# Moving set 2's background windows and lengthening the pause after a set's first pair rows

## The chip, the cores and the metric

One Trainium2 chip, one of its cores. The metric is the device time of one execution in microseconds (us), lower is better. The core has a matrix engine (PE), a vector engine (DVE), a scalar engine (ACT), a general engine (POOL) and a DMA-issuing queue (SP, "SPq" in the trace); each works its instructions off in program order and waits where an operand is not ready. ACT and POOL can start transfers too; here POOL starts those of the weights and of the `arena` stores.

## The reference

Four batches of eight heads (32 head streams), 768 tokens, head width 40. For each head a 40x40 state is carried along the tokens, and its readings are the tokens' rows of a two-layer feed-forward block:

```python
for t in range(S):
    y[:, :, t] = einsum('bhd,bhde->bhe', r_t, state)
    Sa = einsum('bhde,bhe->bhd', state, a_t)
    state = state * w_t - einsum('bhd,bhe->bhde', Sa, b_t) + einsum('bhd,bhe->bhde', v_t, k_t)
x = y as (tokens, 320)
h = x @ w_in                      # 3072 x 2048
g = h if h >= 1; 0 if h <= -1; else (h + 1)**2 / 4
out = g @ w_out                   # 3072 x 320
```

## The kernel before, in words

The tokens go in 24 **chunks** of 32 steps, each in two halves of 16 heads, so that one chunk's recurrence becomes a handful of small matrix products (lines 482 to 584: `p`, `cg`, `ss`, `x`, `pr`), with one inverse of a 32x32 unit triangular matrix per head and chunk (`tinv`). Four chunks are a **set**, numbered 0 to 5. What does not depend on the state is done a set ahead, in the background, in three jobs per set:

- **rows** (`prelude`, lines 249 to 301, four parts): loads of w, a, k, b (`ld_w`, `ld_a`, `ld_k`, `ld_b`, L261, SP), a copy to `wz` on ACT (L269), two scans and two small operations on DVE (L245, L277, L278), a copy into `arena` on ACT (L279), three products into `arena` on POOL (L280, L289, L296), and one transfer of `arena` to the DRAM buffer `scr` of that set (L297, POOL). `arena` and `wz` exist once, so part p+1's L279 waits until part p's `arena` has left, and part p+1's L269 until part p's L296 has read `wz`.
- **ab** (`ab_set`, lines 315 to 345): per chunk one load of the pair rows from `scr` into `tiab` (four transfers, L313, SP), then per half two transposes `ea` on DVE (L326), 32 small matmuls on PE (L335), and their copy to `pairs` on ACT (L341). `tiab` exists once: the next chunk's load waits for the last transposes of the chunk before. For set 2 two pads of `tiab` on ACT (L120) come ahead.
- **inv** (`invert`, L347): one transpose of `pairs` on DVE (L351), then 31 pairs of operations on POOL (L362, L368). At the set's first chunk `adopt` (L372) takes the result.

The feed-forward block runs beside it, from the readings of earlier chunks: groups of 64 tokens, each in eight steps of 16 matmuls on PE (L628), the gate on ACT and DVE (L636, L637, L639), a split of `gt` into `gh` (ACT, L645) and `gl` (POOL, L646), and 12 matmuls on PE (L658, eight from `gh`, four from `gl`). A group's readings are relaid by SP into `X0` or `X1` (`X<-Y`, L602, L608, L611), its result is stored by SP (L663). Until about 221 us `X1` also serves as scratch for turning the weights into their high and low parts (ACT L720, L724, L740; DVE L728; POOL L741).

What sets the order is a generator scheme. Each job is a generator whose `yield`s name costs, and `background(n)` steps, at point n (ten units to a chunk), whichever job is most behind its share of its window:

```python
due.append((key, s, at, size[key] * (gone(n) - gone(a)) / (gone(b) - gone(a))))
...
key, _, at, _ = max(due, key=lambda x: x[3] - x[2][0])
at[0] += next(back[key])
```

`WINDOWS` gives a and b per job and set (first entry is set 1), so entry 2 belongs to set 2. A larger cost at a `yield` makes the job count as further on, hence leaves it alone for longer; the size of a job is the sum of its costs. In `ab_set` the pause between the first load of a set and its first transposes is one such cost:

```python
load_rows(tiab, 4 * s, O_A, 80)
yield AB_W[5]
...
if c < 4 * s + 3:
    load_rows(tiab, c + 1, O_A, 80)
    yield AB_W[4]
```

A window only moves the *program order* on each engine; how long anything takes is the chip's.

Of the kernel before, what the change touches and what calls it, by code (L numbers as in the profile page):

```python
# [25 lines left out]


WINDOWS = dict(
    rows=[(0, 0), (24, 43), (46, 64), (70, 90), (106, 130)],
    ab=[(0, 0), (46, 55), (68, 84), (95, 119), (135, 159)],  # L30
    inv=[(5, 36), (55.5, 79), (85, 118), (121, 158), (161, 198)],
)

AHEAD = 5
# [3 lines left out]
SLOTS = len(SHARE)  # L38

ROWS_W = (2, 2, 4, 2, 6, 6, 8)  # L40
AB_W = (1, 16, 1, 4, 46, 40)
INV_W = 12

TRAIL = 2.5
# [10 lines left out]
def rwkv_moe_kernel(ctx: ExitStack, tc: tile.TileContext, r, k, v, w, a, b, w_in, w_out, ident_d, mask_d, out):  # L55
# [247 lines left out]
    def load_rows(dst, c, off, n, h0=0, nh=NH):  # L303

        sc = scr[c // 4]
        for f in range(2):
            for q in range(2):
                row = (h0 + f) * 128 + 32 * (c % 4)
                m = n - 32 * q
                src = bass.AP(  # L310
                    sc.tensor, sc.offset + row * RW + off + 32 * q, [[RW, 32], [256 * RW, nh // 2], [1, m]]
                )
                nc.sync.dma_start(dst[64 * f + 32 * q : 64 * f + 32 * q + 32, :, 0:m], src)  # L313

    def ab_set(s):
# [3 lines left out]
        load_rows(tiab, 4 * s, O_A, 80)  # L319
        yield AB_W[5]  # L320
        for c in range(4 * s, 4 * s + 4):
            tv = tiab.rearrange("p h (j x) -> p h j x", x=40)[:, :, :, 0:32]
            for half in range(2):
                ea = work.tile([128, 8, 2, 32], F32, tag="ea", name="ea")
                for i in range(2):
                    nc.vector.transpose(ea[:, 4 * i : 4 * i + 4], tv[:, 8 * half + 4 * i : 8 * half + 4 * i + 4])  # L326
                    yield AB_W[0]
                yield AB_W[1]
                ps = psum()[:, 0:128]
# [11 lines left out]
                nc.scalar.copy(pairs_f[:, at : at + 128], ps)  # L341
                yield AB_W[2] + AB_W[3]
# [4 lines that stand above are left out]
# [32 lines left out]
    def staged(key, needs, work_of):  # L379
        for s in range(2 if key != "inv" else 0, NS):  # L380
            if needs:
                drain(needs, s)
            total = 0
            for d in work_of(s):
                total += d
                yield d
            if s:
                size[key] = total
            done[key] = s
            yield 0  # L390

    turned_in, turned_out = set(), set()
    done, size, spent = dict(rows=1, ab=1), dict(rows=10 + 4 * (1 + sum(ROWS_W)), ab=AB_W[5] + 3 * AB_W[4] + 8 * (2 * AB_W[0] + sum(AB_W[1:4])), inv=INV_W + 67), {}
    back = {k: staged(*a) for k, a in dict(
# [570 lines left out]
```

## Time and profile before

| | |
|---|---|
| time, median of 3 runs | 860.29 us (860.02 to 860.31) |
| the profiled execution: its own time | 861.24 us |
| its span, first to last instruction | 859.4 us |
| mean granted PE clock | 0.883 of full |
| busy share PE / DVE / ACT / POOL | 80% / 69% / 49% / 51% |

The sum in the prediction is made in the profiled execution's time, which lies 0.95 us above the median of the timed runs; 1.84 us of it are around the span. A busy share is an average: PE is nearly always busy in the last third and has its holes before.

### The profile page before, as it was taken

The numbers are of one execution on the slowest core, as the hardware profiler recorded it, in microseconds if no ns is written. First come the engines' busy times: TensorE is split into PE (matmuls) and PEld (weight loads), VectorE is DVE, ScalarE is ACT, GpSimd is POOL, SyncE is SP. The second block draws the span as 40 slices with busy tenths as digits, with TensorE's granted clock in tenths as the row PEclk, the third lists the DMA queues.
The fourth block names the chain that finished last, engine by engine and source line by source line (L and its number), as shares of the span: only waits on it lengthen the run. The fifth ranks groups of instructions, "written<-read, shape, count | busy, mean of one in ns | idle before, by whom it ended". The sixth has DMA issues, their size and how long they took to land.

```text
span 859.4 us, 35431 instructions
## 1 busy us (share of the span) xinstructions
PE 690.8 (80%) x15360; PEld 633.3 (74%) x15360; DVE 594.3 (69%) x1338; ACT 417.5 (49%) x888; POOL 441.8 (51%) x621
## 2 busy tenths in 40 slices
PE   4225656687567877878998889999999999999994
PEld 4224545576456866768887789898898999999994
DVE  6895689888556845787677797677876778676210
ACT  6306455557433533445545455455455555555552
POOL 0300279986232677845678548674267742222331
PEclk9665656788786989879999799999999999999998
DMA  8999599987598666986858976667354456350100
GB/s 291 188 198 233 95 194 206 217 196 184 130 172 149 152 156 112 181 189 150 165 127 165 190 179 154 131 130 134 85 111 89 98 106 131 84 119 23 36 16 16
DMA packets 221459, 122.01 MB, mean 142 GB/s; under 512 B 142144, under 2 KB 214016, under 8 KB 221304
## 3 DMA queue, kind: packets, MB, share of 16 engines
q1 hardware_dynamic: 215032, 98.12, 56.6%
q0 software_dynamic: 6272, 21.63, 9.4%
q8 instruction: 121, 1.98, 1.1%
q14 instruction: 34, 0.28, 0.1%
HBM read 90.54 MB, written 27.53 MB: 137 GB/s over the span
## 4 chain that ended last, share of the span: by engine, by line
PE 42%; DMA 10%; DVE 6%; POOL 5%; ACT 3%; SPq 3%; issue 2%; ACTq 0%; DVEq 0%; POOLq 0%
PE ph L628 14%; PE po L658 13%; PE p L553 4%; DMA ti<-scr 3%; PE p L542 3%; SPq L313 3%; DMA tiab<-scr 2%; PE p L516 2%; PE p L582 2%; PE p L482 2%; PE p L526 2%; DMA ld_b<-in_b_dram 2%; DMA scr<-arena 2%; POOL gl L646 1%; POOL lw L368 1%
## 5 line engine op out<-in xcount | busy, mean ns | idle before, releaser
L646 POOL TENSOR_TENSOR gl<-gt,gh 128x512 fp32r<-128x512 f32 x96 | 123.8, 1290 | 204.5 <-ACT gh L645 204.5
L628 PE MATMUL ph<-X,w 120*128 120x256 f32 x1536 | 219.1, 296 | 1.2 <-issue 1.2
L628 PEld LDWEIGHTS ph<-X,w 120*128 120x128 f32 x1536 | 198.7, 198 | 8.3 <-issue 1.7
L658 PE MATMUL po<-w,gh 128*128 128x320 f32 x768 | 135.9, 320 | 19.8 <-ACT gh L645 19.8
L658 PEld LDWEIGHTS po<-w,gh 128*128 128x128 f32 x768 | 117.4, 193 | 23.8 <-ACT gh L645 23.1
L639 DVE SCALAR_TENSOR_TENSOR gt<-gt,ph 128x512 f32<-128x512 f32 x96 | 65.7, 684 | 96.2 <-ACT gt L637 87.2
L537 ACT ACTIVATE cg<-p 32x160 f32<-32x160 f32 x192 | 56.5, 295 | 92.5 <-PE p L526 58.8
L658 PE MATMUL po<-w,gl 128*128 128x320 f32 x384 | 79.7, 332 | 20.7 <-POOL gl L646 20.7
L560 DVE SCALAR_TENSOR_TENSOR cg<-p,pr 40x160 f32<-40x160 f32 x184 | 59.1, 321 | 50.8 <-PE p L553 48.7
L636 ACT ACTIVATE gt<-ph,half_c 128x512 f32<-128x512 f32 x96 | 66.0, 688 | 58.0 <-PE ph L628 58.0
L368 POOL TENSOR_TENSOR lw<-lw 128x31 f32<-128x31 f32 (+15 forms) x155 | 86.6, 559 | 9.4
L362 POOL TENSOR_TENSOR lw<-lw 128x31 f32<-128x31 f32 (+15 forms) x155 | 84.0, 542 | 8.9
L494 DVE TENSOR_TENSOR cg<-p,mask 32x256 f32<-32x256 f32 x192 | 80.6, 420 | 3.5
L658 PEld LDWEIGHTS po<-w,gl 128*128 128x128 f32 x384 | 63.7, 201 | 25.3 <-POOL gl L646 24.9
L553 PE MATMUL p<-cg 128*64 128x72 f32 (+1 forms) x1536 | 66.0, 245 | 0.0
L645 ACT CAST gh<-gt 128x512 fp32r<-128x512 f32 x96 | 59.6, 621 | 10.5 <-DVE gt L639 9.5
L547 ACT COPY ss<-p 40x320 f32<-40x320 f32 x92 | 38.6, 419 | 48.7 <-PE p L542 47.2
L637 ACT ACTIVATE gt<-gt 128x512 f32<-128x512 f32 x96 | 60.7, 632 | 3.1
L553 PEld LDWEIGHTS p<-cg 128*64 128x64 f32 x1536 | 60.4, 154 | 0.4 <-issue 0.4
L533 DVE SCALAR_TENSOR_TENSOR cg<-p,mask 32x128 f32<-32x128 f32 x192 | 55.3, 288 | 6.3 <-PE p L526 1.1
L582 PEld LDWEIGHTS p<-pr,ss 40*40 40x40 f32 x1472 | 35.9, 129 | 30.1 <-issue 23.1
L582 PE MATMUL p<-pr,ss 40*40 40x32 f32 x1472 | 40.9, 210 | 21.1 <-DVE pr L466 16.3
(94 smaller groups left out, 1058.9 us busy)
## 6 DMA issues: line engine op xcount, KB each, us to landing
ti<-scr SPq DMA_DIRECT2D x96, 200.0 KB
ti<-scr SPq DMA_DIRECT2D x96, 168.0 KB
scr<-arena POOLq DMA_DIRECT2D x16, 640.0 KB, 6.4
cg<-scr SPq DMA_DIRECT2D x96, 80.0 KB
X<-Y SPq DMA_DIRECT2D x36, 160.0 KB
scr<-wide SPq DMA_DIRECT2D x8, 640.0 KB
w<-in_moe_w_out_dram POOLq DMA_DIRECT2D x16, 320.0 KB, 5.2
tiab<-scr SPq DMA_DIRECT2D x32, 160.0 KB
```

What stands on the lines that cost most here:

```text
L362: eng.tensor_mul(t3, W3[:, 0:n, j : j + 1].broadcast_to([128, n, m]), L3[:, j + 1 :, j].unsqueeze(1).broadcast_to([128, n, m]),)
L368: eng.tensor_sub(W3[:, 0:n, j + 1 :], W3[:, 0:n, j + 1 :], t3)
L494: nc.vector.tensor_tensor(out=cg[q, f::2, C_X : C_X + 64][:, 4 * i : 4 * i + 4].rearrange("p h (j x) -> p h j x", x=32), in0=ps[quarter(f, ...
L553: nc.tensor.matmul(psv[h // 8][64 * f : 64 * f + 64, h // 2 % 4, 0:n3], lhsT=cgw[:, h * CW + C_G : h * CW + C_G + 64], rhs=cg[:, h, C_R : ...
L582: nc.tensor.matmul(psv[er[f], p, :], lhsT=ss[er[f], p, :], rhs=pn[er[f], p, 0, 8:40], start=True, stop=True)
L628: nc.tensor.matmul(phs[k % 2][:, n * j : n * j + n], lhsT=wt[0, f // 4, wi // 2][:, wi % 2, fs], rhs=Xs[g][:, xi, :], start=i == 0, stop=i ...
L636: nc.scalar.activation(gt, ph, AF.Relu, bias=half_c, scale=0.5)
L637: nc.scalar.activation(gt, gt, AF.Square)
L639: nc.vector.scalar_tensor_tensor(out=gt, in0=gt, scalar=1.0, in1=ph, op0=ALU.min, op1=ALU.max)
L645: nc.scalar.copy(gh, gt)
L646: nc.gpsimd.tensor_sub(gl, gt, gh.bitcast(F32))
L658: nc.tensor.matmul(pos[i], lhsT=x[:, ts_], rhs=w, start=q == 0 and k == 0, stop=end)
```

## The change

Only the table is edited. Set 2's rows go from 24–43 to 23–41 units (start a tenth of a chunk sooner, end a fifth sooner), its pair rows from 46–55 to 44–57, its inverse from 55.5–79 to 57.5–79; set 3's pair rows start one unit sooner. The cost after the first `tiab` load goes from 40 to 100, in every set from 2 on, so the ab job's size goes from 362 to 422.

```diff
 WINDOWS = dict(
-    rows=[(0, 0), (24, 43), (46, 64), (70, 90), (106, 130)],
-    ab=[(0, 0), (46, 55), (68, 84), (95, 119), (135, 159)],
-    inv=[(5, 36), (55.5, 79), (85, 118), (121, 158), (161, 198)],
+    rows=[(0, 0), (23, 41), (46, 64), (70, 90), (106, 130)],
+    ab=[(0, 0), (44, 57), (67, 84), (95, 119), (135, 159)],
+    inv=[(5, 36), (57.5, 79), (85, 118), (121, 158), (161, 198)],
...
-AB_W = (1, 16, 1, 4, 46, 40)
+AB_W = (1, 16, 1, 4, 46, 100)
```

No instruction is added or removed; they stand in another order. Three places, on two engines, follow (`scr2` is the buffer of set 2, `scr3` of set 3).

SP, where set 2's first pair rows (chunk 8) are loaded. Before:

```order
L602 DMA X1_2929<-Y_618 40x1024 x3
L608 DMA X1_2929<-Y_618 40x2x256 x2
L611 DMA X1_2929<-Y_618 40x2x256
L313 DMA tiab_81<-scr2_107 32x16x80
L313 DMA tiab_81<-scr2_107 32x16x48
L313 DMA tiab_81<-scr2_107 32x16x80
L313 DMA tiab_81<-scr2_107 32x16x48
L261 DMA ld_w_3029<-in_w_dram 128x1x320
```

And after the change:

```order
L313 DMA tiab_81<-scr2_107 32x16x80
L313 DMA tiab_81<-scr2_107 32x16x48
L313 DMA tiab_81<-scr2_107 32x16x80
L313 DMA tiab_81<-scr2_107 32x16x48
L602 DMA X1_2935<-Y_618 40x1024 x3
L608 DMA X1_2935<-Y_618 40x2x256 x2
L611 DMA X1_2935<-Y_618 40x2x256
L261 DMA ld_w_3029<-in_w_dram 128x1x320
```

The load has moved ahead of the relayout of `X1`; set 3's `ld_w` stands behind both, as before.

DVE, around the transposes of set 2's second and third loads (`ea<-tiab`; chunks 9 and 10). Before:

```order
L466 STREAM_TRANSPOSE pr2_90<-ti1_83 128x16x32
L326 STREAM_TRANSPOSE ea_3346<-tiab_81 128x256 x2
L326 STREAM_TRANSPOSE ea_3386<-tiab_81 128x256 x2
L326 STREAM_TRANSPOSE ea_3414<-tiab_81 128x256 x2
L245 SCALAR_TENSOR_TENSOR ld_w_3224<-wz_79,dz_80 128x400
L277 COPY dz_80<-ld_w_3224 128x40
L278 RECIPROCAL dz_80<-ld_w_3224 128x40
L245 SCALAR_TENSOR_TENSOR wz_79<-wz_79,dz_80 128x400
L639 SCALAR_TENSOR_TENSOR gt_3418<-gt_3418,ph1_64 128x512
L584 SCALAR_TENSOR_TENSOR cg2_87<-p2_3463,pr0_88 40x8x32 x2
```

And after the change:

```order
L466 STREAM_TRANSPOSE pr2_90<-ti1_83 128x16x32
L326 STREAM_TRANSPOSE ea_3327<-tiab_81 128x256 x2
L326 STREAM_TRANSPOSE ea_3361<-tiab_81 128x256 x2
L245 SCALAR_TENSOR_TENSOR ld_w_3224<-wz_79,dz_80 128x400
L277 COPY dz_80<-ld_w_3224 128x40
L278 RECIPROCAL dz_80<-ld_w_3224 128x40
L245 SCALAR_TENSOR_TENSOR wz_79<-wz_79,dz_80 128x400
L639 SCALAR_TENSOR_TENSOR gt_3394<-gt_3394,ph1_64 128x512
L326 STREAM_TRANSPOSE ea_3414<-tiab_81 128x256 x2
L584 SCALAR_TENSOR_TENSOR cg2_87<-p2_3420,pr0_88 40x8x32 x2
```

Before, the first row of `ea` behind L466 is chunk 9's second half and the next two are chunk 10's; after, both rows behind L466 are chunk 9's, and chunk 10's first half comes behind the scans and the gate operation L639. Its second half is now behind `cg<-ti` L461, five operations on.

SP, around set 2's fourth load (chunk 11). Before:

```order
L261 DMA ld_k_3411<-in_k_dram 128x1x320
L313 DMA tiab_81<-scr2_107 32x16x80
L313 DMA tiab_81<-scr2_107 32x16x48
L313 DMA tiab_81<-scr2_107 32x16x80
L313 DMA tiab_81<-scr2_107 32x16x48
L142 DMA scr3_108<-in_v_dram 4096x1x40
L261 DMA ld_b_3458<-in_b_dram 128x1x320
L261 DMA ld_w_3461<-in_w_dram 128x1x320
```

And after the change (the copy L142, `ld_b`, `ld_w`, four `ti1` loads and four `cg0` loads now precede these rows):

```order
L445 DMA cg0_85<-scr1_106 32x8x40
L261 DMA ld_a_3555<-in_a_dram 128x1x320
L313 DMA tiab_81<-scr2_107 32x16x80
L313 DMA tiab_81<-scr2_107 32x16x48
L313 DMA tiab_81<-scr2_107 32x16x80
L313 DMA tiab_81<-scr2_107 32x16x48
L261 DMA ld_k_3680<-in_k_dram 128x1x320
```

The fourth load has moved back past eleven transfers, to behind `ld_a`.

On ACT the rows job of set 2 moves too: L269 and L279 of its parts 1 to 3, which stood behind L645 (`gh<-gt`) or close to it, stand a feed-forward step sooner; and the two pads L120 go from behind the L645 at 221.54 us to ahead of the L636 at 218.77 us. In sets 4 and 5 the first transposes of `tiab` on DVE stand one chunk half later behind their load, and the third and fourth loads of `tiab` stand later on SP; in set 4 the fourth goes from ahead of the `ti` and `cg` loads to behind the following `ld_k`, in set 5 from ahead of the `ti` and `cg` loads to behind them.

## Rows read from the trace of the kernel before

**Rows 1.** Busy time by stretch of the span: from and to, length, busy time of PE, its weight loads, DVE, ACT, POOL (instructions), granted PE clock, DMA share, GB/s.

```profile
140.00:225.00 85.00, 61.59 (x1200) 55.08 (x1200) 71.12 (x138) 51.21 (x116) 68.24 (x90) 0.83 0.86 193
225.00:300.00 75.00, 51.64 (x1156) 46.91 (x1160) 46.14 (x99) 26.92 (x60) 27.37 (x33) 0.77 0.76 156
...
620.00:859.00 239.00, 225.61 (x4398) 212.42 (x4392) 137.10 (x328) 123.21 (x255) 97.56 (x120) 0.99 0.35 76
```

**Rows 2.** Waits over the whole span: engine, what waited, for what: us in total, times, longest us.

```profile
DVE ea L326 <- DMA tiab<-scr: 31.3, 6, 13.6
PE p L335 <- DVE ea L326: 29.2, 8, 11.7
ACT arena L279 <- DMA scr<-arena: 14.6, 5, 4.9
```

**Rows 3.** Timeline of PE: start us, us, engine, line and operation, in brackets the idle time before it and what ended it.

```profile
232.43 0.68 PE L335 MATMUL p<-ea 40*32 40x32 f32 x32 [8.25 <-DVE ea L326]
238.31 3.46 PE L628 MATMUL ph<-X,w 120*128 120x256 f32 x16
248.74 0.56 PE L335 MATMUL p<-ea 40*32 40x32 f32 x32 [1.51 <-DVE ea L326]
262.99 0.76 PE L335 MATMUL p<-ea 40*32 40x32 f32 x32 [11.70 <-DVE ea L326]
278.64 2.18 PE L628 MATMUL ph<-X,w 120*128 120x256 f32 x16
310.80 1.43 PE L658 MATMUL po<-w,gl 128*128 128x320 f32 x4 [5.38 <-POOL gl L646]
```

**Rows 4.** Timeline of SP's queue, 221 to 270 us: start us, us to issue, line, transfer, how many.

```profile
221.44 2.46 SPq L602 DMA_DIRECT2D X<-Y  x3
...
225.65 0.77 SPq L611 DMA_DIRECT2D X<-Y  x1
226.59 1.95 SPq L313 DMA_DIRECT2D tiab<-scr  x4
228.58 0.61 SPq L261 DMA_DIRECT2D ld_w<-in_w_dram  x1
...
250.74 6.46 SPq L313 DMA_DIRECT2D tiab<-scr  x4
...
264.62 1.94 SPq L313 DMA_DIRECT2D tiab<-scr  x4
...
277.70 0.54 SPq L261 DMA_DIRECT2D ld_a<-in_a_dram  x1
```

**Rows 5.** Timeline of DVE, same columns as rows 3.

```profile
231.84 0.77 DVE L326 STREAM_TRANSPOSE ea<-tiab 128x256 f32<-128x256 f32 x2 [7.99 <-DMA tiab<-scr]
...
234.72 0.99 DVE L245 TENSOR_TENSOR_SCAN ld_w<-wz,dz 128x400 f32<-128x400 f32 x1
...
262.49 0.77 DVE L326 STREAM_TRANSPOSE ea<-tiab 128x256 f32<-128x256 f32 x2 [13.57 <-DMA tiab<-scr]
...
268.34 0.85 DVE L584 SCALAR_TENSOR_TENSOR cg<-p,pr 40x256 f32<-40x256 f32 x2
...
279.99 0.67 DVE L466 STREAM_TRANSPOSE pr<-ti 128x512 f32<-128x512 f32 x1
```

**Rows 6.** The chain that ended last, 255 to 425 us: start us, us, what.

```profile
255.97 6.39 DMA tiab<-scr
...
421.37 3.95 DMA tiab<-scr
```

**Rows 7.** Timeline of ACT, 156 to 225 us.

```profile
164.30 0.76 ACT L269 COPY wz<-ld_w 128x320 f32<-128x320 f32 x1 [2.12 <-POOL arena L296]
...
170.61 0.78 ACT L279 COPY arena<-ld_w 128x320 f32<-128x320 f32 x1 [4.90 <-DMA scr<-arena]
...
205.08 0.80 ACT L279 COPY arena<-ld_w 128x320 f32<-128x320 f32 x1 [1.29 <-DMA scr<-arena]
...
218.77 0.68 ACT L636 ACTIVATE gt<-ph,half_c 128x512 f32<-128x512 f32 x1
```

**Rows 8.** Transfers of the tile `arena` to DRAM: us from issue to landing; and the page's row of them with the size of one.

```profile
DMA to landing us min/median/max: 4.2/6.4/9.4
scr<-arena POOLq DMA_DIRECT2D x16, 640.0 KB, 6.4
```

**Rows 9.** The page's groups of the inverse's two operations: busy us, mean ns of one, idle before.

```profile
L368 POOL TENSOR_TENSOR lw<-lw 128x31 f32<-128x31 f32 (+15 forms) x155 | 86.6, 559 | 9.4
L362 POOL TENSOR_TENSOR lw<-lw 128x31 f32<-128x31 f32 (+15 forms) x155 | 84.0, 542 | 8.9
```

**Rows 10.** Timeline of DVE in sets 4 and 5, same columns as rows 3.

```profile
425.51 0.77 DVE L326 STREAM_TRANSPOSE ea<-tiab 128x256 f32<-128x256 f32 x2 [3.47 <-DMA tiab<-scr]
...
484.42 0.73 DVE L326 STREAM_TRANSPOSE ea<-tiab 128x256 f32<-128x256 f32 x2
...
544.22 0.77 DVE L326 STREAM_TRANSPOSE ea<-tiab 128x256 f32<-128x256 f32 x2 [3.78 <-DMA tiab<-scr]
```

**Rows 11.** Timeline of PE, behind the first of the waits in rows 10.

```profile
427.77 0.46 PE L335 MATMUL p<-ea 40*32 40x32 f32 x32 [0.24 <-DVE cg L584]
```

**Rows 12.** Timeline of SP's queue around set 4's fourth load.

```profile
467.35 5.38 SPq L313 DMA_DIRECT2D tiab<-scr  x4
...
480.27 0.55 SPq L261 DMA_DIRECT2D ld_k<-in_k_dram  x1
```

## The prediction

> **What bounds the kernel now.** I read the busy time by stretch first. From 620 us on PE is busy for 225.61 of 239 us at a granted clock of 0.99 [rows 1]: no hole to speak of, so whatever comes earlier or later before that point passes one for one to the end. In the stretch 225 to 300 us it is busy for only 51.64 of 75 us, at 0.77 [rows 1]. The change reorders work in and around it. Next the list of waits: DVE waits 31.3 us in six places for the pair rows of `tiab`, and PE 29.2 us in eight places for the transposes made of them [rows 2]. The timeline of PE shows where: 8.25 us before 232.43, 1.51 before 248.74, 11.70 before 262.99, together 21.46 us, all in set 2 [rows 3]. DVE's own waits behind the first and the last of these are 7.99 and 13.57 us, and both end with a landing of `tiab<-scr` [rows 5]. So the hole is two late loads, passed DVE to PE. While it lasts the clock falls to 1.2 GHz: the 16 matmuls at 238.31 take 3.46 us, those at 278.64 take 2.18 [rows 3].
>
> A second wait matters, since the change touches it: ACT waits 14.6 us in five places for `arena` to have left [rows 2].
>
> **First load of set 2 (chunk 8).** Now SP relays `X1` from 221.44 to 226.42, then issues the load at 226.59, and DVE goes on at 231.84 [rows 4, 5], 5.25 us after the first issue. DVE had come to the wait at 231.84 − 7.99 = 223.85. After the change the load stands ahead of the relayout. It then waits for the two pads, which ACT makes just before the L636 at 218.77 [rows 7]; with their 1.2 us and the rows job shifted I put the issue at 220.0 to 222.0, landing 5.25 behind the first issue, at 225.3: a wait of 1.4 us instead of 7.99. That would be 6.6 us, but DVE does not keep it. Behind the transposes comes the scan of set 3's first part, at 234.72, 2.88 us behind 231.84 [rows 5]; it would come to 228.2. Its `ld_w` is issued behind load and relayout in both orders: 228.58 now [rows 4], 227.0 then (222.0 plus the relayout's 4.98). The fastest landing of a comparable transfer is 3.95 us [rows 6], and now at most 234.72 − 228.58 = 6.14 with ACT's copy in it. With 3.95 and a copy of 0.76 [rows 7] the scan starts at 231.7: **−3.0 us**, between −1.6 (6.14) and −6.6 (it has long landed). What stands behind the scan on DVE (L584, then the masks, which PE and ACT wait for) moves with it. So `ld_w` is what is late next.
>
> **Third load (chunk 10).** It keeps its place behind the stores of `ob`; its four issues take 6.46 us from 250.74 because the queue is full [rows 4], and the last lands 6.39 us after 255.97 [rows 6]. It lands about as late as now, less what the stretch before gained. But what stands behind the wait changes: now DVE makes both halves' transposes, two scans, their small operations and a gate operation before it reaches L584 at 268.34, 5.85 us after the wait ended at 262.49 [rows 5]. After the change scans and gate stand ahead of the wait and are made inside it; between the wait and L584 is one pair of transposes, 0.77. So L584, and with it the recurrence, gains 5.08: **−5.0 us**. The bounds: nothing, if the scan's `ld_w` or ACT's copy of it is late too (the second load now stands ahead of that `ld_w` on SP); 11.7, if the wait goes whole. I take the value the DVE rows give, since the load's place on SP is the same. With the stalls shorter by 8 us of some 21, one group of 16 matmuls goes at 2.4 GHz: 3.46 − 2.18, **−1.3 us** (0 to −2.6).
>
> **Fourth load (chunk 11).** Now issued at 264.62, it is never waited for. Afterwards it stands behind the copy of v, four `ti1` and four `cg0` loads and `ld_a`, which goes out at 277.70 today [rows 4], about 9 us sooner by then: issue 269 to 271, landing 5.25 to 8.3 us behind the first issue (1.94 + 6.39 with the third load's landing), at 274.3 to 277.3. Its transposes stand behind the L466 at 279.99 [rows 5], then at 271.4 (279.99 + 0.67 − 9.3). DVE waits 3 to 6 us, and L351, the next scan and the gate with it: **+3.5 us**, between 0 (`ti` and `cg` need less time when the queue is less full) and 6. This is a wait that the change makes.
>
> **The rows job sooner, 150 to 215 us.** ACT makes L269 and L279 of parts 1 to 3 one step ahead. L269 waits for POOL's L296 (2.12 us before 164.30) and L279 for `arena` to leave (4.90 before 170.61, 1.29 before 205.08) [rows 7]. These waits stood behind the L645 of their step; now the L645, the L547 and the weights stand behind them. A transfer of `arena` lands 4.2 to 9.4 us after its issue, 6.4 in the middle [rows 8]. PE is busy for 61.59 of 85 us there [rows 1], so part of it is cover. If each of the three waits for `arena` is one middle landing less what ACT does meanwhile (some 3 us), and half lies in PE's holes, that is 3 × 3.4 / 2 = 5; less what is already paid for two of the parts (4.90 and 1.29, half) 3.1, so 2; with three waits of 2.12 for L296, of which one is paid, another 1: **+3.0 us**, from 0 to 12.7 (three times 2.12 + 4.90, 21.06, less the 8.31 paid today, all of it on PE's path). By the Trainium skill ("DMA: Bandwidth & Descriptors", section "Anatomy of one DMA — SWDGE (gpsimd) path") a transfer that POOL starts takes about 2.0 us and its bytes over 436 GB/s: an estimate of 3.5 us for 655,360 bytes. The trace disagrees: its fastest is 4.2 and its middle 6.4 [rows 8]. By the Trainium skill the waits for `arena` would nearly vanish and the total be some 3 us less; I keep the rows.
>
> **POOL behind set 2's inverse.** At 310.80 PE has waited 5.38 us for `gl` [rows 3], which stood behind operations of the inverse. The inverse starts later, so three of its pairs fewer stand ahead, 3 × (0.559 + 0.542) [rows 9]: **−3.3 us** (0 to −5.4). The same pairs come later in a window of 21.5 units instead of 23.5, up to 340 us, where PE waits for `gl` again: **+1.0 us** (0 to 3.3).
>
> **Sets 3 to 5.** DVE's waits of 3.47 and 3.78 us at the first loads [rows 10] go, as the transposes stand half a chunk later. PE hardly had them: 0.24 us before the products at 427.77 [rows 11]. Against that set 4's fourth load goes from 467.35 to behind `ld_k` at 480.27 [rows 12], and its transposes are due at 484.42 [rows 10]: landing 5.25 us after an issue at 480.8 gives 486.1, a new wait of 1.6 us; set 5 has the like, with more room. **+1.0 us** (−1.5 to +4).
>
> **Sum.** −3.0 − 5.0 − 1.3 + 3.5 + 3.0 − 3.3 + 1.0 + 1.0 = **−4.1 us**: gains of 12.6, losses of 8.5. The profiled execution's 861.24 becomes 857.1, and the timed median, 860.29, becomes **856.2**.
>
> **Rivals.** *The waits go whole.* If the loads land in time everywhere and none is late in their place, PE gets back 21.46 and the clock's 1.3 and POOL's 3.3, less 5.0 of losses without the fourth load's: −21.1, 839.2. For it speaks that the first load has three times its cover; against it that third and fourth load go no sooner on SP. *A new wait takes the place of the old.* `ld_w` of set 3 is as late as `tiab` was (−3.0 becomes 0) and the fourth load costs 6: gains 9.6, losses 11.0, 861.7, within what a measurement can tell from no change. For it speaks that it is the same queue and the same bytes; in that case the change does not do what moving the first load says. *The rows job's ring decides, slower.* With the waits of L269 and L279 all on the path, 12.7 instead of 3.0: 12.6 − 18.2 = −5.6 the wrong way, 865.9. It decides from the point where they cost more than 3.0 + 4.1 + 1.7 = 8.8. For it speaks that each L645 feeds PE directly and ACT is strictly in order; against it that PE had 23 us of holes there anyway. *The stores of `arena` land before ACT asks for them*: the 3.0 of the ring is nothing, 853.2; the fastest landing, 4.2 us [rows 8], is longer than the some 3 us of ACT's work between, so I give it little. (It is what the Trainium skill's figure above would make of it.)
>
> **How the numbers follow.** Two runs of this kernel can be told apart from about 0.2%, 1.7 us. The sum's case has 0.45 (its own range 850 to 858.5), the early landing 0.03, the waits gone whole 0.10; no measurable change 0.18; the ring (or late loads of sets 4 and 5 with it) 0.24. Faster is 0.58, same 0.18, slower 0.24. The range of 847 to 866 leaves out the waits gone nearly whole and the worst of the ring.
>
> **What would show it.** In the trace after: DVE's wait at the first load of set 2 falls below 3 us, and the scan behind it waits for `ld_w`; at the third load DVE still waits for `tiab`, with scan and gate ahead of it; a new wait of 3 to 6 us for `tiab` at the fourth load; ACT's waits at L279 between 155 and 200 us grow and stand ahead of L645; PE's wait before 310 for `gl` shrinks to about 2; around 484 us DVE waits for `tiab`. The prediction is wrong if the third load lands 5 us sooner or later than now apart from the shift, or if the stretch to 225 us ends over 6 us later.

## The result, and the profile after

| | before | after |
|---|---|---|
| median of 13 runs each | 860.31 us (856.06 to 863.92) | 867.03 us (861.53 to 871.52) |
| ratio, 95% interval | | 1.0078 (1.0049 to 1.0107) |
| the profiled execution, its span | 861.24, 859.4 us | 869.86, 868.0 us |

The change makes the kernel 0.8% slower; 856.2 was forecast, with 866 as the upper end. The first three runs of before lay within 0.3 us of each other, thirteen spread over 8: one profiled execution is good to some us, so a reading below counts only where its step is larger than that or is seen in several kernels. The two profiled executions compared here differ by 8.6 us, the medians by 6.7. The ratios of this document leave out two runs that lie over 1.5% above the fastest of their kernel (one of the pause alone, one of the earlier `ld_w` in the changed kernel), so they are not always the quotients of the medians.

Busy time by stretch of the kernel after, to be set beside [rows 1]:

```profile
140.00:225.00 85.00, 57.79 (x1160) 52.07 (x1154) 65.11 (x131) 45.29 (x105) 66.54 (x89) 0.77 0.85 189
225.00:300.00 75.00, 57.16 (x1187) 51.35 (x1182) 46.91 (x107) 31.68 (x70) 27.21 (x29) 0.82 0.84 162
...
620.00:859.00 239.00, 232.62 (x4580) 218.73 (x4577) 144.35 (x343) 126.35 (x262) 99.38 (x122) 1.00 0.38 80
```

In the hole of 225 to 300 us PE is busy 57.16 us instead of 51.64, as the change meant. From 140 to 225 it is busy 57.79 us instead of 61.59.

The same program point can be followed through both traces: the start of the n-th `gh` copy (L645 on ACT), of which both have 96. The difference after − before, worked out from their starts:

| copy of `gh` | before, us | after − before | what lies in between |
|---|---|---|---|
| 1st | 161.56 | +9.69 | rows of set 2, part 1 |
| 7th | 221.54 | +8.05 | rows of set 2, parts 2 and 3, and the pads L120 |
| 11th | 279.07 | −2.50 | set 2's first to third load: 10.55 gained |
| 13th | 295.48 | +1.95 | set 2's fourth load: 4.45 lost |
| 15th | 316.87 | −0.33 | POOL's `gl`: 2.28 gained |
| 29th | 434.55 | +1.60 | set 3: 1.93 lost |
| 51st | 593.76 | +7.74 | sets 4 and 5: 6.14 lost, 5.67 of it by the 36th |
| 95th | 842.48 | +8.62 | the rest |

Waits over the whole span, after, to be set beside [rows 2]:

```profile
PE po L658 <- ACT gh L645: 31.5, 13, 8.6
PE p L335 <- DVE ea L326: 25.1, 10, 6.2
ACT arena L279 <- DMA scr<-arena: 20.8, 7, 5.4
ACT wz L269 <- DMA ld_w<-in_w_dram: 20.7, 4, 6.1
DVE ea L326 <- DMA tiab<-scr: 15.2, 5, 5.8
```

and two lines of the kernel before that the rows ahead don't have:

```profile
PE po L658 <- ACT gh L645: 19.8, 16, 4.1
ACT wz L269 <- DMA ld_w<-in_w_dram: 3.7, 2, 3.6
```

DVE's wait for `tiab` is halved, from 31.3 to 15.2 us, but PE's wait for the transposes falls only from 29.2 to 25.1. In its place PE waits 11.7 us more for `gh`, which ACT makes, and ACT waits 17.0 us more for `ld_w`.

### The profile page after: what moved, and what is told of

The parts are those of the page before. It is cut to its first block, busy times and chain, and to the rows that moved or that the text cites. A ratio compares the mean times of both kernels' runs of the same rounds, so it can differ in the third digit from the quotient of the medians.

```text
span 868.0 us, 35424 instructions
## 1 busy us (share of the span) xinstructions
PE 694.7 (80%) x15360; PEld 637.2 (73%) x15360; DVE 589.8 (68%) x1338; ACT 418.2 (48%) x888; POOL 442.9 (51%) x621
## 4 chain that ended last, share of the span: by engine, by line
PE 39%; DVE 4%; POOL 4%; DMA 3%; ACT 2%; issue 2%; SPq 1%; ACTq 0%; POOLq 0%; DVEq 0%
PE ph L628 13%; PE po L658 12%; PE p L553 3%; PE p L542 2%; PE p L516 2%; PE p L582 2%; DMA ti<-scr 2%; PE p L482 2%; PE p L526 2%; POOL gl L646 1%; POOL lw L368 1%; POOL lw L362 1%; PE p L335 1%; ACT gh L645 1%; DVE lw L351 1%
## 5 line engine op out<-in xcount | busy, mean ns | idle before, releaser
L658 PE MATMUL po<-w,gh 128*128 128x320 f32 x768 | 139.8, 325 | 31.5 <-ACT gh L645 31.5
L658 PEld LDWEIGHTS po<-w,gh 128*128 128x128 f32 x768 | 120.7, 199 | 35.3 <-ACT gh L645 34.6
L639 DVE SCALAR_TENSOR_TENSOR gt<-gt,ph 128x512 f32<-128x512 f32 x96 | 65.5, 682 | 96.5 <-ACT gt L637 83.1
L636 ACT ACTIVATE gt<-ph,half_c 128x512 f32<-128x512 f32 x96 | 66.0, 688 | 62.0 <-PE ph L628 61.8
L658 PE MATMUL po<-w,gl 128*128 128x320 f32 x384 | 79.5, 331 | 11.8 <-POOL gl L646 11.7
L645 ACT CAST gh<-gt 128x512 fp32r<-128x512 f32 x96 | 59.6, 621 | 10.5 <-DVE gt L639 9.5
L582 PEld LDWEIGHTS p<-pr,ss 40*40 40x40 f32 x1472 | 36.7, 132 | 29.2 <-issue 22.8
```

Source lines behind the costliest of these rows:

```text
L582: nc.tensor.matmul(psv[er[f], p, :], lhsT=ss[er[f], p, :], rhs=pn[er[f], p, 0, 8:40], start=True, stop=True)
L636: nc.scalar.activation(gt, ph, AF.Relu, bias=half_c, scale=0.5)
L639: nc.vector.scalar_tensor_tensor(out=gt, in0=gt, scalar=1.0, in1=ph, op0=ALU.min, op1=ALU.max)
L645: nc.scalar.copy(gh, gt)
L658: nc.tensor.matmul(pos[i], lhsT=x[:, ts_], rhs=w, start=q == 0 and k == 0, stop=end)
```

## The experiments

The change has three parts: **rows** (set 2's rows window), **windows** (those of ab for sets 2 and 3 and of inv for set 2) and **pause** (40 to 100). The kernels of one batch ran on one chip and share the runs of the kernel before; its medians in the four batches are 860.31, 860.56, 860.52 and 860.94 us.

**Rows undone.**

```diff
-    rows=[(0, 0), (23, 41), (46, 64), (70, 90), (106, 130)],
+    rows=[(0, 0), (24, 43), (46, 64), (70, 90), (106, 130)],
```

> Set 2's rows back in their old window (24 to 43), all else as changed. Theory R (the earlier rows put ACT's L269 and L279 ahead of L645, and that costs 8 us by the time of the seventh gh, 221.5 us): the first eight gh lie within 1.5 us of the kernel before, PE's waits for gh of 8.62 and 7.09 us before 207 us fall back to about 1 and 4, and the time is 867.0 - 8 = 859, plus up to 2 because the first pair rows now find the rows job just finished: 859 to 861. Theory C (the loss by 221 us is the lower granted clock of that execution, 0.54 against 0.63 from 100 to 140 us, not the order): the time stays at 865 to 869.

Measured: 862.75 us, ratio to before 1.0029 (1.0005 to 1.0053). The 1st and 7th `gh` lie +0.36 and +1.81 us from before, not +9.69 and +8.05. Theory R holds for the place: PE waits for `gh` 1.28 and 3.71 us before 200 us, where it waited 1.28 and 4.07 in the kernel before. The 1.81 has a cause of its own: up to the 6th `gh` the difference is +0.43, and then ACT makes the two pads of `tiab` (L120, 1.24 us), which the new window of ab puts ahead of the 7th. The other three kernels with rows in the old window, the new window of ab and one buffer show the same step of 1.4 us, and those without that window don't. The time misses 859 to 861, as something later loses more than I allowed; the profiled execution (866.96) is the longest of its twelve, so its later differences can be some 4 us too large.

**Pause undone.**

```diff
-AB_W = (1, 16, 1, 4, 46, 100)
+AB_W = (1, 16, 1, 4, 46, 40)
```

> The pause after a set's first pair rows back at 40, the new windows kept. Theory P (the pause is what costs about 5 us in sets 4 and 5, by loads 3 and 4 that come too late): the drift of the gh against the kernel before between 420 and 600 us, +4.6 us in the changed kernel, falls to 0 to 1; the 8 us by 221 us stay; set 2 keeps a part of its gain of 10.5 us. The time is 861 to 864. Rival (the drift in sets 4 and 5 follows from the delay that set 2 hands on, not from the pause): the drift stays, 865 to 869.

Measured: 860.56 us, 1.0005 (0.9985 to 1.0025). The 7th `gh` stays late (+8.24); between the 29th and the 51st the difference goes from −0.53 to −3.84, no loss. Theory P holds for the place; the drift is below its 0 to 1, and the time just under its 861 to 864. (The profiled execution, 857.58, is the shortest of the twelve.)

**Rows alone,** on the kernel before:

```diff
-    rows=[(0, 0), (24, 43), (46, 64), (70, 90), (106, 130)],
+    rows=[(0, 0), (23, 41), (46, 64), (70, 90), (106, 130)],
```

> The kernel before with set 2's rows at 23 to 41 alone. Theory R: the first eight gh are 6 to 9 us late, as in the changed kernel, and the gain of 10.5 us at the first and third loads of set 2 is not there, since the pair rows keep their window: 866 to 870. Theory C: no delay by 221 us, 859 to 862.

Measured: 865.77 us, 1.0049 (1.0030 to 1.0069). The 1st and 7th `gh`: +8.54 and +4.58. The time is just under theory R's 866 to 870, and the 7th `gh` under its 6 to 9; the gain in set 2 is not there, as it said (+6.02 at the 11th). That the early delay comes without the other two parts, at a granted clock of 0.63 from 100 to 140 us as in the kernel before (after: 0.54), rules theory C out.

**Pause alone,** on the kernel before:

```diff
-AB_W = (1, 16, 1, 4, 46, 40)
+AB_W = (1, 16, 1, 4, 46, 100)
```

> The kernel before with the pause of 100 alone. Theory P: sets 4 and 5 lose about 5 us as in the changed kernel; set 2's first load gets twice its cover but its later loads less, so it gains 0 to 6: 859 to 865, and the drift of the gh between 420 and 600 us is +4 to +6. Rival: no drift there (0 to 1), and set 2's gain alone shows: 854 to 860.

Measured: 866.90 us, 1.0056 (1.0021 to 1.0090), outside both ranges. The loss is not in sets 4 and 5 first: between the 15th and the 27th `gh` (set 3) the difference goes from −1.73 to +7.75, then from +6.23 at the 29th to +8.64 at the 51st (sets 4 and 5). In set 2 nothing is lost: +1.70 at the 7th, −1.60 at the 11th, −1.73 at the 15th. The profiled execution (870.79) is among the longest of the twelve (858.74 to 871.85), so the sizes are rough.

**What the early rows wait for.** `tiab` is as large as `arena` and unused between about 70 us and set 2's pair rows. Parts 1 and 3 of set 2 use it, so their L279 need not wait until the part before has left:

```diff
+            other = tiab.rearrange("p h x -> p (h x)")
+            R = (other if s == 2 and part % 2 else arena).rearrange("p (t x) -> p t x", x=160)
+            kt, P, at, bt = (R[:, :, 40 * i : 40 * i + 40] for i in range(4))
```

On the changed kernel:

> The changed kernel, with parts 1 and 3 of set 2's rows written to the buffer of tiab (as large, and unused until 220 us) instead of arena, so that L279 of set 2's parts no longer waits for a store of arena to leave; the order on all engines stays. Theory R1 (the early delay of 8 us comes from the waits of L279 for the landing, 5.18 and 5.43 us, now ahead of L645): the delay at the seventh gh falls to 2 to 4 us and the time to 861 to 864. Theory R2 (it comes from L269's waits for L296, 1.54, 3.94 and 1.48 us, and from L279 standing behind a late scan): the delay stays at 6 to 9 us, 866 to 868.

Measured: 863.52 us, 1.0040 (1.0017 to 1.0064), and the 7th `gh` at +2.45 instead of +8.05. ACT's timeline of the kernel after:

```profile
161.18 0.81 ACT L269 COPY wz<-ld_w 128x320 f32<-128x320 f32 x1 [1.54 <-POOL arena L296]
169.05 0.77 ACT L279 COPY arena<-ld_w 128x320 f32<-128x320 f32 x1 [5.18 <-DMA scr<-arena]
171.25 0.62 ACT L645 CAST gh<-gt 128x512 fp32r<-128x512 f32 x1
179.34 0.77 ACT L269 COPY wz<-ld_w 128x320 f32<-128x320 f32 x1 [3.94 <-POOL arena L296]
...
203.78 0.76 ACT L279 COPY arena<-ld_w 128x320 f32<-128x320 f32 x1 [5.43 <-DMA scr<-arena]
206.12 0.62 ACT L645 CAST gh<-gt 128x512 fp32r<-128x512 f32 x1
```

PE's, right behind, in the kernel after:

```profile
171.93 2.50 PE L658 MATMUL po<-w,gh 128*128 128x320 f32 x8 [8.62 <-ACT gh L645]
...
206.79 2.50 PE L658 MATMUL po<-w,gh 128*128 128x320 f32 x8 [7.09 <-ACT gh L645]
```

and in the kernel before:

```profile
162.24 1.45 PE L658 MATMUL po<-w,gh 128*128 128x320 f32 x8 [1.14 <-ACT gh L645]
...
198.60 2.50 PE L658 MATMUL po<-w,gh 128*128 128x320 f32 x8 [4.07 <-ACT gh L645]
```

And ACT's with the second buffer, where the line numbers behind the edit are one higher:

```profile
163.37 0.79 ACT L280 COPY tiab<-ld_w 128x320 f32<-128x320 f32 x1
165.58 0.62 ACT L646 CAST gh<-gt 128x512 fp32r<-128x512 f32 x1
...
197.15 0.76 ACT L280 COPY tiab<-ld_w 128x320 f32<-128x320 f32 x1 [1.21 <-DVE ld_w L245]
201.09 0.62 ACT L646 CAST gh<-gt 128x512 fp32r<-128x512 f32 x1
```

Without the wait for the landing the first `gh` starts at 165.58 instead of 171.25; PE's two waits are then 2.30 and 4.59 us instead of 8.62 and 7.09. Of the 8.05 us of early loss the second buffer takes back 5.6: those are the waits of L279 for `arena` to leave. Of the 2.45 left some 1.4 can be the pads, which cost as much in kernels without the earlier rows; what remains for L269 behind L296 (theory R2), about 1 us, can't be told from the spread of single profiles. Theory R1 holds. By medians the buffer is worth 3.5 us (867.03 − 863.52).

The same buffer in the kernel before:

> The kernel before with the same second buffer for set 2's parts 1 and 3. Its waits of L279 for landings, 4.90 and 1.29 us before 206 us, go. If they were covered (they stand behind L645 there): 859.5 to 861. If they cost PE as they cost ACT: 855 to 858.

Measured: 858.41 us, 0.9972 (0.9953 to 0.9991), at the edge of the second range and in neither. So those waits, 6.2 us on ACT, were mostly covered there, and cost some 2 us.

**The windows alone.**

```diff
-    ab=[(0, 0), (46, 55), (68, 84), (95, 119), (135, 159)],
-    inv=[(5, 36), (55.5, 79), (85, 118), (121, 158), (161, 198)],
+    ab=[(0, 0), (44, 57), (67, 84), (95, 119), (135, 159)],
+    inv=[(5, 36), (57.5, 79), (85, 118), (121, 158), (161, 198)],
```

> The kernel before with the new windows of ab and inv alone (set 2's rows as before, pause 40). Theory S (the three parts add up: rows +4.4, pause +5.5, windows of ab and inv -4): 856 to 858. Rival (the windows gain only if the rows end sooner or the pause is longer, since the first pair rows need both): 860 to 862.

Measured: 853.38 us, 0.9919 (0.9896 to 0.9942): faster than both kernels, and by more than theory S gave. The 15th `gh` lies 7.90 us ahead of before, and the lead stays (8.08 at the 55th). By the medians of this and the runs above, rows cost 860.56 − 853.38 = 7.2 us on top of it, the pause 862.75 − 853.38 = 9.4; both together 13.7, less than their sum. DVE in set 2 of this kernel, at the first and at the third load:

```profile
225.54 0.77 DVE L326 STREAM_TRANSPOSE ea<-tiab 128x256 f32<-128x256 f32 x2
...
259.37 0.77 DVE L326 STREAM_TRANSPOSE ea<-tiab 128x256 f32<-128x256 f32 x2 [8.48 <-DMA tiab<-scr]
```

The windows alone take away the wait at the first load (7.99 us before) and leave most of that at the third (8.48 instead of 13.57). With the pause the third is waited for 3.68 us, but DVE waits at the second and fourth loads instead (2.38 and 5.81; rows further on).

**Where the pause costs.** The windows with a pause of 100 in set 2 alone, first, then in set 3 alone (the job's size is corrected for the sets behind):

```diff
-        yield AB_W[5]
+        yield AB_W[5] if s == 2 else 40
...
-                size[key] = total
+                size[key] = total - 60 if (key, s) == ("ab", 2) else total
```

> As the run with rows back in their old window (862.75), but the pause of 100 in set 2 alone and 40 in sets 3 to 5. Theory P (the pause costs in sets 3 to 5): the gh lie 2 to 6 us ahead of the kernel before at 317 us as there, and keep it: 856 to 859. Rival (it costs in set 2, by its late fourth load): 861.5 to 864.

Measured: 856.67 us, 0.9951 (0.9933 to 0.9969), inside theory P's range, but 3.3 us behind the windows alone. Its difference from before goes from −7.73 at the 11th `gh` to −3.31 at the 13th, behind the fourth load, and back to −7.22 at the 15th; so this trace doesn't show where in set 2 or after it the 3.3 us lie.

```diff
-        yield AB_W[5]
+        yield 100 if s == 3 else 40
...
-                size[key] = total
+                size[key] = total + {("ab", 2): 60, ("ab", 3): -60}.get((key, s), 0)
```

> The new windows of ab and inv alone (853.38), with the pause of 100 in set 3 alone. Theory W: PE's wait for the transposes near 340 us appears again, and the time is 856 to 859. Rival (the pause costs in sets 4 and 5 alone): 853 to 854.5.

Measured: 856.34 us, 0.9946 (0.9920 to 0.9973), inside theory W's range, 3.0 us behind the windows alone. By medians the pause's 9.4 us are thus 3.3 in set 2, 3.0 in set 3, and 3.1 left for sets 4 and 5. These shares are rough: the intervals of both runs overlap that of the windows alone, and the 3.1 was not measured but is what is left if the shares add up, which the three parts above did not. Theory W shows in the rows. The changed kernel, DVE in set 3:

```profile
341.20 0.99 DVE L245 TENSOR_TENSOR_SCAN ld_w<-wz,dz 128x400 f32<-128x400 f32 x1 [4.74 <-ACT wz L269]
```

ACT, which that scan waits for:

```profile
340.41 0.76 ACT L269 COPY wz<-ld_w 128x320 f32<-128x320 f32 x1 [5.51 <-DMA ld_w<-in_w_dram]
```

PE, which waits for the transposes behind the scan (the view ends inside this group of 32):

```profile
344.56 0.66 PE L335 MATMUL p<-ea 40*32 40x32 f32 x24 [6.20 <-DVE ea L326]
```

and PE with the pause in set 3 alone, which in the windows alone has no wait there:

```profile
336.15 0.76 PE L335 MATMUL p<-ea 40*32 40x32 f32 x32 [5.71 <-DVE ea L326]
```

In the kernel before both halves' transposes stood ahead of this scan; DVE waited there for the same `ld_w` (3.75 us before 340.63), but PE's next rows were not the products of transposes behind it. The pause moves the second half's transposes to behind the scan, and a late load of the rows job, which was covered, reaches PE.

**The late `ld_w` taken away,** in the changed kernel (the first `ld_w` of a set from 3 on goes out when the set before has done with the buffer):

```diff
-        wl, al, kl = load("w", 0), load("a", 0), load("k", 0)
+        wl = next_w.pop(s) if s in next_w else load("w", 0)
+        al, kl = load("a", 0), load("k", 0)
...
             if part < 3:
                 wl = load("w", part + 1)
+            elif s + 1 < NS:
+                next_w[s + 1] = load("w", 0, s + 1)
```

> The changed kernel, with the first ld_w of each set's rows from set 3 on issued at the end of the rows of the set before (its buffer is free then) instead of at the start of its own. Theory W (in set 3 the pause puts the second half's transposes behind a scan that waits for this ld_w, and PE, in order, waits 6.20 us at 344 us for them): ACT's wait of 5.51 us for ld_w before 340 us goes, PE's 6.20 us falls to 0 to 2, and the time from 867.0 to 859 to 863. Rival (something else is late in its place, or the wait was covered): 865 to 868.

Measured: 865.81 us, 1.0030 (1.0003 to 1.0058), against 1.0078 (1.0049 to 1.0107) for the change: the time misses 859 to 863 and lies in the rival's range, and the intervals overlap, so a gain is not shown. PE in sets 2 and 3 of this kernel (line numbers five higher):

```profile
253.82 0.68 PE L340 MATMUL p<-ea 40*32 40x32 f32 x32 [9.04 <-DVE ea L331]
...
283.06 0.68 PE L340 MATMUL p<-ea 40*32 40x32 f32 x32 [5.53 <-DVE ea L331]
337.97 0.65 PE L340 MATMUL p<-ea 40*32 40x32 f32 x32 [1.30 <-DVE ea L331]
```

The 6.20 us at 344 have become 1.30, and ACT no longer waits there for `ld_w`: what stood behind what is shown. But PE waits 9.04 us at set 2's second load, where it waited 3.42 in the changed kernel: that load is issued only 1.1 us sooner, and DVE comes to it 6.7 us sooner. The local wait is settled; its price in time isn't. And the edit doesn't touch a wait in set 4 that all kernels with the pause there have (see "Sets 3 to 5" below), since it moves only the first `ld_w` of a set.

**Together.** The windows with the second buffer:

> The new windows of ab and inv alone (853.38) with the second buffer for set 2's parts 1 and 3 as well. If the 2.1 us that this buffer gave the kernel before add up: 850 to 852.5. If they come from the same hole that the windows filled: 853 to 854.5.

Measured: 853.02 us, 0.9895 (0.9857 to 0.9932), just inside the second range; no difference from the windows alone can be told. With the earlier `ld_w` too:

> As the run before this, with the earlier ld_w too. Theory W also holds without the pause (the scan of set 3's rows waits for ld_w at 231 us there, 4.67 us on ACT): 1 to 4 us less than that run, 847 to 851. Rival (without the pause no transposes stand behind those scans, so the wait is covered): within 1 us of that run.

Measured: 848.48 us, 0.9862 (0.9819 to 0.9904), inside theory W's range: the fastest measured, 1.4% under the kernel before. Against 853.02 the intervals overlap, so that the earlier `ld_w` adds is not shown. (The 4.67 us of the expectation were read in the kernel with the pause in set 2; in the windows alone that wait is 1.11 us.) PE still waits 10.65 us at set 2's third load in this kernel, before 260.08: the larger half of the hole is open.

## Why the prediction was wrong, point by point

The prediction got the hole in set 2 right, and two costs far too small. Of its own signs of being wrong, one came true: the stretch to 225 us ends over 6 us later (8.05 at the 7th `gh`).

**First and third load.** −3.0, −5.0 and −1.3 were forecast, 9.3 together; between the 7th and the 11th `gh` 10.55 are gained. DVE in set 2 after the change:

```profile
237.97 0.99 DVE L245 TENSOR_TENSOR_SCAN ld_w<-wz,dz 128x400 f32<-128x400 f32 x1 [4.08 <-ACT wz L269]
...
254.26 0.77 DVE L326 STREAM_TRANSPOSE ea<-tiab 128x256 f32<-128x256 f32 x2 [2.38 <-DMA tiab<-scr]
...
266.45 0.77 DVE L326 STREAM_TRANSPOSE ea<-tiab 128x256 f32<-128x256 f32 x2 [3.68 <-DMA tiab<-scr]
...
283.97 0.77 DVE L326 STREAM_TRANSPOSE ea<-tiab 128x256 f32<-128x256 f32 x2 [5.81 <-DMA tiab<-scr]
```

The first load isn't waited for, against 7.99 us [rows 5]; the scan behind it waits, through ACT's L269, for `ld_w`, as forecast; the third load is still waited for, 3.68 us instead of 13.57, with scan and gate ahead of it. The wait of 2.38 at the second load was not foreseen. That the sum came near doesn't show its shares, and is in part luck: in the windows alone, which gain 7.5 us over the same stretch, PE's wait at the first load falls from 8.25 to 2.77 us and at the third only from 11.70 to 9.54; the pause alone gains 3.3.

**Fourth load.** +3.5 forecast with a wait of 3 to 6 us: 5.81 us on DVE, and 4.45 us lost by the 13th `gh`. Right.

**POOL.** −3.3 forecast, 2.28 gained; PE's wait before `gl`, 5.38 us [rows 3], is:

```profile
310.43 1.44 PE L658 MATMUL po<-w,gl 128*128 128x320 f32 x4 [2.82 <-POOL gl L646]
```

**The rows job sooner: the step that failed first.** The mechanism was right and the term too small: +3.0 was forecast, +8.05 stood at the 7th `gh` (some 6.5 without the pads), and by medians the earlier rows cost 4.3 to 7.2 us, by what stands beside them (867.03 − 862.75 in the change, 865.77 − 860.56 alone, 860.56 − 853.38 on the windows). Two of its sizes were off. A wait for a landing was put at 3.4 us; the two that came were 5.18 and 5.43. L279 started 7.6 and 7.1 us after the issues of those stores, at 161.45 and 196.72, where 6.4 was taken, and ACT came to it 2.4 and 1.6 us after them, not 3. And 3.1 us were taken off as paid already; that was about 2 us, as the second buffer in the kernel before showed (2.1 by medians). Letting half of the waits fall into PE's holes was not far off: the 10.61 us of these two cost 5.6. A slip of 1 us goes the same way: the paid wait for L296 is taken off whole where the paid waits for landings are halved. Part 2 waited for its late scan, 4.53 us before 186.74, and not for a landing.

By the Trainium skill ("DMA: Bandwidth & Descriptors", section "Anatomy of one DMA — SWDGE (gpsimd) path") a store of `arena` takes 3.5 us, an estimate. That fares worse than the rows: the median landing after the change is 6.7 us:

```profile
scr<-arena POOLq DMA_DIRECT2D x16, 640.0 KB, 6.7
```

**Sets 3 to 5: the step that failed second.** With the inverse's +1.0, +2.0 was forecast and 8.95 measured (from the 15th `gh` to the end: 8.62 + 0.33; the profiled pair lies 1.9 us further apart than the medians). The term asked only whether a load of `tiab` lands too late and what PE had of DVE's old waits. The late fourth load in set 4 cost DVE 0.8 us in all between 440 and 520 us, less than the 1.6 forecast. What cost was not in the list: waits for `ld_w` that the pause makes, or that it puts in front of something PE needs.

In set 3 the rows show the second kind: transposes that were moved behind a scan, on an engine in order, take over that scan's wait (6.20 us on PE). Little of it is left at the 29th `gh`: from the 15th the changed kernel loses 1.93 us, with the pause undone 1.24, with the earlier `ld_w` 1.75. In the other kernels with the pause in set 3 it is 3.5 to 8.0, so what that wait costs differs from kernel to kernel.

The loss is in set 4, 5.67 us from the 29th to the 36th `gh`. There ACT's L269 waits for `ld_w` ahead of the 35th. Before:

```profile
473.94 0.80 ACT L269 COPY wz<-ld_w 128x320 f32<-128x320 f32 x1 [0.16 <-DMA ld_w<-in_w_dram]
```

And after the change:

```profile
481.33 0.77 ACT L269 COPY wz<-ld_w 128x320 f32<-128x320 f32 x1 [6.09 <-DMA ld_w<-in_w_dram]
```

PE then waits 2.47 us for `gh` at 488.92. The pattern holds over the kernels here: the five with a pause of 100 in set 4 (the change, rows undone, pause alone, the change with the second buffer, the change with the earlier `ld_w`) wait 5.74 to 6.52 us at this L269 and lose 2.6 to 6.4 us from the 29th to the 36th `gh`; the eight others, which have a pause of 40 there, wait at most 1.74 us for `ld_w` at it and lose nothing. So the pause causes both the wait and the loss; that the loss is this wait, and not something else of the pause in set 4, was not tested by itself.

**The rivals.** The ring's case, priced at 865.9 with 12.7 instead of 3.0, named the right mechanism for the early loss; it was to decide from 8.8, and 8.05 alone would have left the kernel level. With sets 3 to 5 it came out at 867.03. The range's upper end, 866, took each loss singly; they came together.

## What to carry to other kernels

A row that is moved on an engine in order takes over the wait of whatever it is moved behind, and hands it to its own reader: for each moved row read which row ahead of it waits, and for what, not only whether its own operand is late. Where one buffer links two steps (here `arena`), bringing the second step nearer to the first turns a covered transfer into a wait: here 5.2 and 5.4 us of the 7.6 and 7.1 from issue to the next write. And a table of windows that helps in one part may hide losses in two others: the windows here were worth about −7 us alone, and rows and pause +7 and +9 on top of them (+5 and +6 on the kernel before), and only taking them singly showed it.

## What the runs showed that was not expected

Thirteen executions of the kernel before spread from 856.06 to 863.92 us, where three had lain within 0.3; a difference of a few us needs many executions, not a single profile. And the granted clock went with PE's waits in the two kernels, down from 0.83 [rows 1] to 0.77 from 140 to 225 us and up from 0.77 to 0.82 from 225 to 300. But with the rows undone PE is busier from 225 to 300 us (60.56 us) at a lower clock (0.75), so what the clock adds to a stall or gives back stays open.
